# A planned attention-plus-MLP kernel: layer norms, diagonal masks, copies of V and output halves moved between engines, and a new order of all instructions

## The chip, the cores and the metric

The kernel runs on one core of a Trainium2 chip. The metric is the device time of one execution in microseconds (us). It was taken in five runs of the kernel before; the median is 239.56 us, the lowest 237.9 and the highest 241.4. One more execution was recorded by the hardware profiler.

The engines are named as in the profile: PE is TensorE (matmuls), DVE is VectorE, ACT is ScalarE, POOL is GpSimd, and SP issues nearly all transfers. "PEld" is the weight load of PE. "SPq" marks work of SP's queue.

## The reference

```python
x = A_x                                  # 2048 x 512, bf16
xn = layernorm(x)
out = x + A(xn, wq, wk, wv, wo, beta) + silu(xn @ w1) @ w2      # w1: 512 x 1792

# A: 32 heads of 16 columns; 4 segments of 512 rows, one after the other
q, k, v = xn @ wq, xn @ wk, xn @ wv      # split by head and segment
M, z = 0, 0
for s in range(4):
    p = softmax(qs @ ks.T / 4 + causal mask)      # inside the segment
    a_dot = p @ vs
    a_mem = (phi(qs) @ M) / (phi(qs) @ z + 1e-6)  # phi(t) = t + 1 if t > 0 else exp(t)
    o_s = g * a_mem + (1 - g) * a_dot             # g = sigmoid(beta)
    M, z = M + phi(ks).T @ vs, z + sum(phi(ks))
A = concat(o_s) @ wo
```

## The kernel before

**Order.** The kernel does not run its steps in the order in which they are written. `Plan.build` makes the operations, each with an engine, an occupancy and a latency in ns, the data it reads and writes, and a rank out of the list `PRIO` (1,162 numbers). `Plan.schedule` (L1071) plays them through a small model of the five engines and four PSUM banks and writes down one fixed order; each engine's queue then holds its instructions in that order, with semaphores between engines. So every change of a cost or a rank can change the order of the whole kernel. The model has a rule for DVE and POOL: an operation of DVE marked `port` that starts while POOL is busy is prolonged to the end of POOL's operation, and the reverse (L1137 to L1145).

**Front.** x of segment 0 is loaded in two halves, then wk, wq, wv, w1, x of segment 1, w2 and wo (L353 to L362). While these come, PE runs 51 products of an identity (`warm`, L446). The layer norm (`ln`, L454) takes tiles of 128 rows: `bn_stats` and `bn_aggr` on DVE (L477, L478) for mean and variance, or, for tile 3 of segment 0, three activations on ACT (L461 to L468); adding eps and raising to -0.5 on POOL (L486, L489); the normalization itself on DVE (L496). Segment 0 is transposed by PE (L508) and copied out of PSUM by ACT (L520), with 6 filling products behind each transposition; the others are transposed by a DMA (L525).

**Attention.** Head dimension 16 lets four heads share PE, in four row groups. One set of scores fills a PSUM tile `psS` of 128 x 2048 (four banks), of which there is a single one: PE writes scores (L686), ACT takes the exponential of all 2048 columns into a bf16 tile (L697), and only then may PE write the next scores. There are 64 such rounds (16 groups of eight heads times four) and 8 more for the half tiles at the diagonal, two groups at a time (`halves`, L806, with the exponential at L832 into the single buffer `Pd`). The causal part of each diagonal block is zeroed on POOL by `affine_select`: two of 128 x 256 for each of the 64 (L703), and four for each of the 8, of which two cover 64 and two cover 128 partitions, 1024 columns each (L840).

P times V runs in four column groups (L717) with a column of ones in V, so that row 16 of each group is the softmax's sum. V is kept as 16 pairs of heads, 2 heads of a pair, 16 + 1 columns (`K.V`); `low` copies the lower 64 rows of one head of each pair into VA (L608) and of the other into VB (L609), on DVE, 16 times. The two results of a group are copied out of PSUM by DVE into `No` (L749) and `N` (L753); the last `N` alone is copied by ACT.

**Division.** SP's queue gathers the rows of sums (L763) and merges `No` into `N` (L774). DVE inverts the sums and multiplies by the gate (`rc`, L784 and L785); a store to DRAM (L794) and a replicating load (L802) spread the reciprocals over partitions, and DVE multiplies (L964, or L953 in segment 0). The same is done for the memory's denominator (L866 to L870, L877, L885, L890).

**The rest.** q and k are copied out of PSUM by DVE (L543, L584); POOL makes masked copies of k (`kTo`, L548, L556). phi takes ACT (exp, L618), POOL (min, L622) and DVE (L628, with a running sum for k). w1's products go through tanh on ACT (L648) and a product on DVE (L654) into hT; w2 and wo are products of 14 and 4 steps, all issued by a helper (L91 with the full array, L96 in column groups).

```python
op("PE", 222, 228, sc, tau(n) - 700, ..., w=[("psS", n)], mode="R", kind="S")
K.nc.scalar.activation(out=pt(K)[:], in_=K.psS[:], func=AF.Exp, scale=SCALE)      # L697
K.nc.gpsimd.affine_select(out=a, in_=a, compare_op=ALU.is_ge, fill=0.0, base=64 * h,
                          pattern=[[0, 16], [1, 64]], channel_multiplier=-1)      # L840
```

## Time and profile before

| | |
|---|---|
| five runs | 241.4, 237.9, 239.56, 239.55, 239.59 us; median 239.56 |
| the profiled execution's own time | 237.94 us, 1.62 below that median |
| its span, first to last instruction | 236.0 us, so 1.94 us lie around it |
| granted TensorE clock | 1.000 |
| DVE busy | 189.5 us of the span (80%), 336 instructions |
| bytes moved | 18.70 MB; HBM read 11.53 MB, written 2.33 MB |
| SP's queue | rows of issues cover 160.9 us of 236.0 |

How to read it: "busy" is the union of an engine's instructions. Consecutive instructions of ACT, and of DVE, overlap a little in the record, since the end of one is written while the next has begun. In a timeline row the columns are start, duration (both us), engine, line, operation, what it writes and reads, shape, count, and in brackets the idle time before it and what ended that. A row with a count of several merges neighbours. An instruction that cannot get what it needs after it was issued is shown as longer, not as waiting.

### The profile page before, as it was taken

To read this page: it belongs to the slowest core of one execution; us is meant where nothing else is said; L and a number is where in the kernel's file an instruction comes from. 1 tells how busy PE (TensorE), PEld (TensorE's weight loads), DVE (VectorE), ACT (ScalarE), POOL (GpSimd) and SP (SyncE) were. 2 spreads that over 40 slices of the span, in tenths; PEclk is the share of its full clock that TensorE was granted. 3 is DMA by queue.
4 is the path that set the end of the run, shared out by engine and by line. 5 is a ranking of instruction groups with operands and counts; after the bars stand their busy time and mean duration, and the time that the engine had idled before them with its cause. 6 is when DMAs were issued, how large, how long until landed. Compare 5 with 4: busy or idle time off the path is not lost.

```text
span 236.0 us, 8073 instructions
## 1 busy us (share of the span) xinstructions
PE 219.5 (93%) x3378; PEld 104.5 (44%) x3378; DVE 189.5 (80%) x336; ACT 182.6 (77%) x169; POOL 147.9 (63%) x290
## 2 busy tenths in 40 slices
PE   7798979999989999979995999999989999999994
PEld 6733334454344444443441445443434444445541
DVE  3489998999888799699799788979898587783741
ACT  4469999898998999968994768898878889891112
POOL 3389898997956986676767273698739543830000
PEclk9999999999999999999999999999999999999999
DMA  6999451221230211131312212210211200231202
GB/s 195 353 373 267 108 70 31 52 27 37 49 56 19 92 29 35 45 110 57 72 29 52 96 37 68 58 47 10 77 62 40 83 15 15 74 97 36 82 25 89
DMA packets 29356, 18.70 MB, mean 79 GB/s; under 512 B 15753, under 2 KB 28809, under 8 KB 29321
## 3 DMA queue, kind: packets, MB, share of 16 engines
q1 hardware_dynamic: 29176, 18.07, 28.6%
q8 instruction: 26, 0.43, 0.7%
q10 hardware_dynamic: 144, 0.13, 0.2%
q14 instruction: 10, 0.07, 0.2%
HBM read 11.53 MB, written 2.33 MB: 59 GB/s over the span
## 4 chain that ended last, share of the span: by engine, by line
PE 46%; DVE 18%; DMA 12%; POOL 7%; SPq 6%; ACT 5%; issue 5%; DVEq 0%; ACTq 0%
PE psb__216 L91 9%; PE psb__214 L91 7%; PE psb__215 L91 6%; DMA x_all<-in_A_x_dram 5%; PE psS L686 5%; PE psb__217 L91 5%; PE psb__215 L96 3%; PE psb__217 L96 2%; SPq L774 2%; DVE rq L785 2%; DMA xnT__89<-xn__87 1%; DVE zr L784 1%; SPq L763 1%; PE psb__216 L96 1%; DMA mrep__189<-dmem__212 1%
## 5 line engine op out<-in xcount | busy, mean ns | idle before, releaser
L840 POOL TENSOR_SCALAR_AFFINE_SELECT Pd__148<-Pd__148 128x1024 bf16<-128x1024 bf16 (+1 forms) x32 | 36.6, 1153 | 8.8 <-ACT Pd__148 L832 8.4
L91 PEld LDWEIGHTS <-w 128*128 128x128 bf16 x169 | 15.3, 98 | 20.6 <-issue 4.3
L697 ACT ACTIVATE Pt__141<-psS 128x2048 bf16<-128x2048 f32 x10 | 18.8, 1880 | 2.9 <-PE psS L686 2.8
L697 ACT ACTIVATE Pt__147<-psS 128x2048 bf16<-128x2048 f32 x9 | 16.9, 1880 | 3.1 <-PE psS L686 2.5
L697 ACT ACTIVATE Pt__146<-psS 128x2048 bf16<-128x2048 f32 x9 | 16.9, 1882 | 2.5 <-PE psS L686 1.9
L697 ACT ACTIVATE Pt__144<-psS 128x2048 bf16<-128x2048 f32 x9 | 16.9, 1880 | 2.2 <-PE psS L686 2.1
L697 ACT ACTIVATE Pt__142<-psS 128x2048 bf16<-128x2048 f32 x9 | 16.9, 1875 | 2.1 <-PE psS L686 2.1
L697 ACT ACTIVATE Pt__145<-psS 128x2048 bf16<-128x2048 f32 x9 | 16.9, 1881 | 0.9 <-PE psS L686 0.7
L697 ACT ACTIVATE Pt__143<-psS 128x2048 bf16<-128x2048 f32 x9 | 16.9, 1877 | 0.7 <-PE psS L686 0.5
L832 ACT ACTIVATE Pd__148<-psS 128x2048 bf16<-128x2048 f32 x8 | 15.0, 1876 | 3.1 <-PE psS L822 2.3
L703 POOL TENSOR_SCALAR_AFFINE_SELECT Pt__147<-Pt__147 128x256 bf16<-128x256 bf16 x18 | 8.2, 470 | 7.0 <-ACT Pt__147 L697 7.0
L703 POOL TENSOR_SCALAR_AFFINE_SELECT Pt__141<-Pt__141 128x256 bf16<-128x256 bf16 x20 | 8.8, 458 | 5.7 <-ACT Pt__141 L697 5.7
L648 ACT ACTIVATE th__170<-psb__217 128x512 bf16<-128x512 f32 x7 | 4.2, 600 | 9.6 <-PE psb__217 L96 9.5
L703 POOL TENSOR_SCALAR_AFFINE_SELECT Pt__143<-Pt__143 128x256 bf16<-128x256 bf16 x18 | 7.6, 438 | 6.1 <-ACT Pt__143 L697 6.0
L703 POOL TENSOR_SCALAR_AFFINE_SELECT Pt__145<-Pt__145 128x256 bf16<-128x256 bf16 x18 | 8.0, 466 | 4.8 <-ACT Pt__145 L697 4.8
L703 POOL TENSOR_SCALAR_AFFINE_SELECT Pt__146<-Pt__146 128x256 bf16<-128x256 bf16 x18 | 7.2, 417 | 4.8 <-ACT Pt__146 L697 4.8
L91 PE MATMUL psb__214<-xnT__89,w 128*128 128x512 bf16 x32 | 9.1, 380 | 1.1 <-DVE hT__150 L654 0.7
L703 POOL TENSOR_SCALAR_AFFINE_SELECT Pt__144<-Pt__144 128x256 bf16<-128x256 bf16 x18 | 7.3, 424 | 4.4 <-ACT Pt__144 L697 4.4
L703 POOL TENSOR_SCALAR_AFFINE_SELECT Pt__142<-Pt__142 128x256 bf16<-128x256 bf16 x18 | 7.6, 435 | 3.2 <-ACT Pt__142 L697 3.2
L96 PEld LDWEIGHTS <-w 128*32 128x32 bf16 x220 | 5.6, 97 | 4.6 <-issue 0.4
L449 PE MATMUL psS<-ident 128*128 128x128 bf16 x75 | 6.3, 250 | 1.4 <-POOL pm L388 1.4
L91 PE MATMUL psb__217<-xnT__90,w 128*128 128x512 bf16 x27 | 7.5, 381 | 0.0
(817 smaller groups left out, 739.5 us busy)
## 6 DMA issues: line engine op xcount, KB each, us to landing
w<-in_B_w_dram SPq DMA_DIRECT2D x2, 1792.0 KB
x_all<-in_A_x_dram SPq DMA_DIRECT2D x8, 256.0 KB
out_dram<-x_all SPq DMA_DIRECT2D x15, 128.0 KB
wk<-in_A_wk_dram SPq DMA_DIRECT2D x1, 512.0 KB
wq<-in_A_wq_dram SPq DMA_DIRECT2D x1, 512.0 KB
wv<-in_A_wv_dram SPq DMA_DIRECT2D x1, 512.0 KB
wo<-in_A_wo_dram SPq DMA_DIRECT2D x1, 512.0 KB
mrep__189<-dmem__211 SPq DMA_DIRECT2D x2, 128.0 KB
```

What stands on the lines that cost most here:

```text
L91: K.nc.tensor.matmul(out, lhsT=lhsT, rhs=rhs, start=start, stop=stop, skip_group_check=True)
L96: K.nc.tensor.matmul(out[32 * g : 32 * g + 32], lhsT=lhsT[:, 32 * g : 32 * g + 32], rhs=rhs, start=start, stop=stop, tile_position=(0, 32 ...
L449: K.nc.tensor.matmul(K.psS[:, 0, 0:P], lhsT=K.ident[:], rhs=K.ident[:], start=True, stop=True)
L648: K.nc.scalar.activation(out=K.th[g % RING["th"]][:], in_=K.bank(t)[:, :], func=AF.Tanh, scale=0.5)
L686: K.nc.tensor.matmul(K.psS[:, g, c : c + L - q0], lhsT=K.kTo[b][r0:r1, kt, 64:192] if par else K.kT[b][r0:r1, kt * P : kt * P + P], rhs=K. ...
L697: K.nc.scalar.activation(out=pt(K)[:], in_=K.psS[:], func=AF.Exp, scale=SCALE)
L703: K.nc.gpsimd.affine_select(out=a, in_=a, compare_op=ALU.is_ge, fill=0.0, base=64, pattern=[[0, 4], [1, 64]], channel_multiplier=-1,)
L763: K.nc.sync.dma_start(out=zt[r : r + 13 : 4, :], in_=src[DH : DH + 97 : 32, 256 * b : 256 * b + 256],)
L774: K.nc.sync.dma_start(out=K.N[nN][r : r + 16, :], in_=K.No[nNo][r - 16 : r, :])
L785: K.nc.vector.tensor_scalar(out=K.rq[0:nr, :], in0=K.zr[0:nr, :], scalar1=K.gcol[0:nr, dts[0] // 3 : dts[0] // 3 + 1], scalar2=None, op0=A ...
L832: K.nc.scalar.activation(out=pd(K)[:], in_=K.psS[:], func=AF.Exp, scale=SCALE)
L840: K.nc.gpsimd.affine_select(out=a, in_=a, compare_op=ALU.is_ge, fill=0.0, base=64 * h, pattern=[[0, 16], [1, 64]], channel_multiplier=-1,)
```

## The change

Work is moved between engines, some constants of the planner are changed, and the order comes from a new `PRIO`:

- First layer norm (segment 0): ACT takes the statistics of tile 1 in place of tile 3; eps is added on DVE; the four normalized tiles have four buffers (two of them the later `oT`) in place of two; tile 2's copy out of PSUM goes to DVE; 47 warming products in place of 51, and 6, 4, 4, 4 filling ones.
- Layer norms of segments 1 to 3: the normalization is one activation on ACT with scale and bias from columns; POOL makes the bias (`shift`) with one small product for each tile.
- The diagonal masks of `halves`: two DVE products for each pair with a 128 x 64 mask `tri` (made once by POOL), repeated over 16 blocks, in place of four `affine_select` on POOL.
- V is kept with the head of the pair ahead of the pair; the copies into VA and VB are 32 transfers on SP's queue in place of 32 copies on DVE.
- All copies into `N` go to ACT; before, 15 of the 16 were on DVE.
- The two gate products after the reciprocals (`rc`, and the one of the memory's denominator) also write an accumulated sum into an unused column `junk`.
- w1 is loaded in two halves; w2, wo and beta are issued after the first k has been copied out.
- The planner: many occupancies and latencies differ by some per cent to some tens of per cent (a masked `halves` score 240 in place of 440 ns, transfers' latencies 1,350 to 1,800 in place of 2,100 to 2,300 ns); a `port` operation of DVE that meets a busy POOL is put aside until POOL's operation, and those marked `port=3` that are queued behind it, have ended.
- `PRIO` is another list of numbers, and so the order of all engines' queues is another.

```diff
-WARM = 51
-FILL = (6, 6, 6, 6)
+WARM = 47
+FILL = (6, 4, 4, 4)
...
+def xn0(K, t):
+    return K.xn[t] if t < 2 else K.oT[t - 2]
...
-        load([("w1",)], ld_w("w1", "B_w1"), 5, 11500)
-        load([("x", 1, 0)], ld_x(1, 0), 6, 12000)
-        load([("x", 1, 1)], ld_x(1, 1), 7, 12500)
-        load([("w2",)], ld_w("w2", "B_w2"), 8, 17000)
-        load([("wo",)], ld_w("wo", "A_wo"), 9, 18000)
+        for h in range(2):
+            load([("w1", h)], ld_w("w1", "B_w1", slice(h * F // 2, (h + 1) * F // 2)), 5 + h, 8500 + 2500 * h)
+        load([("x", 1, 0)], ld_x(1, 0), 7, 11000)
+        load([("x", 1, 1)], ld_x(1, 1), 8, 11500)
+        for i, (name, src) in enumerate((("w2", "B_w2"), ("wo", "A_wo"))):
+            op("SP", 600, 9000 + 3000 * i, ld_w(name, src), 20000 + i, r=[("kT", 0)], w=[(name,)])
...
-        op("SP", 1600, 2300, beta, 30000, w=[("bcol",)], not_before=26500)
+        op("SP", 1900, 6000, beta, 19000, r=[("kT", 0)], w=[("bcol",)])
...
+        def tri(K):
+            K.nc.gpsimd.memset(K.tri[:], 1.0)
+            for n, base in ((P, 64), (64, 0)):
+                K.nc.gpsimd.affine_select(
+                    out=K.tri[0:n, :], in_=K.tri[0:n, :], compare_op=ALU.is_ge, fill=0.0, base=base,
+                    pattern=[[1, 64]], channel_multiplier=-1,
+                )
+        op("POOL", 500, 120, tri, 15500, r=[("kTo", 0, 1)], w=[("tri",)])
...
-            if s == 0 and j == 3:
+            if s == 0 and j == 1:
...
-                op("ACT", 1400, 170, mean, base, r=[("x", s, 1)], w=[("mv", s, j)])
+                op("ACT", 1660, 170, mean, base, r=[("x", s, 0)], w=[("mv", s, j)])
...
+            if s == 0:
+                def eps(K, t=t):
+                    K.nc.vector.tensor_scalar(
+                        out=K.rstd[:, t : t + 2, 0], in0=K.mv[:, t : t + 2, 1], scalar1=EPS,
+                        scalar2=None, op0=ALU.add,
+                    )
+                op("DVE", 70, 130, eps, base + 2000 + 700 * j, r=[("mv", s, j), ("mv", s, j + 1)],
+                   w=[("veps", s, j)])
...
+                if s > 0:
+                    K.nc.gpsimd.tensor_tensor(
+                        out=rs, in0=K.mv[:, t : t + 2, 1], in1=K.lnc[:, 0:2], op=ALU.add
+                    )
                 K.nc.gpsimd.tensor_tensor(out=rs, in0=rs, in1=K.lnc[:, 2:4], op=ALU.pow)
...
+                if s > 0:
+                    for u in (t, t + 1):
+                        K.nc.gpsimd.tensor_scalar(
+                            out=K.shift[:, u : u + 1], in0=K.mv[:, u, 0:1], scalar1=K.rstd[:, u, 0:1],
+                            scalar2=-1.0, op0=ALU.mult, op1=ALU.mult,
+                        )
+            op("POOL", 1270 if s else 520, 150, rstd, base + 2200 + 700 * j,
+               r=([("mv", s, j), ("mv", s, j + 1)] if s else [("veps", s, j)]) + [("lnc",)],
...
+            def norm1(K, j=j, t=t):
+                K.nc.scalar.activation(
+                    out=K.xn[t % RING["xn"]][:], in_=K.x_all[:, t % XT, :], func=AF.Identity,
+                    scale=K.rstd[:, t, 0:1], bias=K.shift[:, t : t + 1],
+                )
+            if s == 0:
+                op("DVE", 322, 190, norm, base + 2500 + 700 * j, port=1,
+                   r=[("x", s, j // 2), ("mv", s, j), ("rstd", s, j)], w=[("xn0", t)])
+            else:
+                op("ACT", 525, 170, norm1, base + 2500 + 700 * j,
+                   r=[("x", s, j // 2), ("mv", s, j), ("rstd", s, j)], w=[("xn", t)])
...
+                    if j == 2:
+                        K.nc.vector.tensor_copy(out=dst, in_=src)
+                    else:
+                        K.nc.scalar.copy(out=dst, in_=src)
+                op("DVE" if j == 2 else "ACT", 590, 150, ev, base + 3000 + 700 * j,
...
-            def low(K, j=j):
-                b = (4 * s + j) % RING["V"]
-                K.nc.vector.tensor_copy(out=K.VA[b][0:64, :, :], in_=K.V[b][0:64, :, 0, :])
-                K.nc.vector.tensor_copy(out=K.VB[b][64:P, :, :], in_=K.V[b][0:64, :, 1, :])
-            op("DVE", 400, 135, low, due + 4000, port=1, r=[("V", 4 * s + j), ("ones", (4 * s + j) % RING["V"])], w=[("VB", 4 * s + j)])
+            for r in range(2):
+                def half(K, j=j, r=r):
+                    b = (4 * s + j) % RING["V"]
+                    K.nc.sync.dma_start(
+                        out=(K.VB if r else K.VA)[b][64 * r : 64 * r + 64, :, :], in_=K.V[b][0:64, r, :, :]
+                    )
+                op("SP", 580, 1700, half, due + 4000, r=[("V", 4 * s + j), ("ones", (4 * s + j) % RING["V"])],
+                   w=[("VB", 4 * s + j, r)])
...
-                f = K.nc.scalar.copy if end else K.nc.vector.tensor_copy
-                f(out=K.N[nN][:], in_=K.bank(tk[0])[:, :])
+                K.nc.scalar.copy(out=K.N[nN][:], in_=K.bank(tk[0])[:, :])
...
-            op("ACT" if end else "DVE", 600, 135, eve, due + 1, r=[("PV", s, dt, 0)], w=[("N", g4, 0)], free=[tk[0]])
+            op("ACT", 480, 160, eve, due + 1, r=[("PV", s, dt, 0)], w=[("N", g4, 0)], free=[tk[0]])
...
-                    scalar2=None, op0=ALU.mult,
+                    scalar2=0.0, op0=ALU.mult, op1=ALU.add, accum_out=K.junk[0:nr, :],
...
-            for h in range(2):
-                def mask(K, di=di, h=h):
-                    a = pd(K)[0 : P if h else 64, :, :].rearrange("p g (j d q) -> p (g j) d q", d=2, q=64)
-                    a = a[:, :, di, :]
-                    K.nc.gpsimd.affine_select(
-                        out=a, in_=a, compare_op=ALU.is_ge, fill=0.0, base=64 * h,
-                        pattern=[[0, 16], [1, 64]], channel_multiplier=-1,
-                    )
-                op("POOL", 1120, 130, mask, tau(n) + 3500 + 5000 * di, r=[("Pd", pr, 0)],
-                   w=[("Pd", pr, 1 + 2 * di + h)], kind="mask")
+            def mask(K, di=di):
+                a = pd(K)[:, :, :].rearrange("p g (j d q) -> p (g j) d q", d=2, q=64)[:, :, di, :]
+                K.nc.vector.tensor_tensor(
+                    out=a, in0=a, in1=K.tri[:, :].unsqueeze(1).broadcast_to([P, 16, 64]), op=ALU.mult
+                )
+            op("DVE", 600, 135, mask, tau(n) + 3500 + 5000 * di, r=[("Pd", pr, 0), ("tri",)],
+               w=[("Pd", pr, 1 + di)], port=1)
...
-                out=K.rec[:], in0=K.zf[:], scalar1=K.gcol[:, 2:3], scalar2=None, op0=ALU.mult
-            )
-        op("DVE", 1650, 135, ev, port=2, due= tau(NQ * s + DUE["den"][s] + 0.3), r=[("psD", s), ("gcol",)], w=[("rec", s)],
+                out=K.rec[:], in0=K.zf[:], scalar1=K.gcol[:, 2:3], scalar2=0.0, op0=ALU.mult,
+                op1=ALU.add, accum_out=K.junk[:],
...
-    K.V = ring("V", [P, H // 2, 2, DH + 1], BF16)
+    K.V = ring("V", [P, 2, H // 2, DH + 1], BF16)
```

## The prediction

> **What bounds the kernel now.** I read the busy shares first, then the table by stretches from the first exponential to the last, then ACT's timeline, then the timelines of the places where ACT stops, then the groups that the change removes. The page's engine shares:
>
> ```profile
> PE 219.5 (93%) x3378; PEld 104.5 (44%) x3378; DVE 189.5 (80%) x336; ACT 182.6 (77%) x169; POOL 147.9 (63%) x290
> ```
>
> No engine but PE looks full, and a busy PE is not one at its peak. The stretches before, between and after the exponentials (13.68 is the start of the first, 211.5 the end of the last; the columns are PE, PEld, DVE, ACT, POOL):
>
> ```profile
> 0.00:13.68 13.68, 10.82 (x141) 9.16 (x142) 6.43 (x14) 5.92 (x11) 5.29 (x25) 1.00 0.85 291
> 13.68:211.50 197.82, 187.94 (x2830) 84.36 (x2832) 172.08 (x307) 172.70 (x152) 141.85 (x263) 1.00 0.27 67
> 211.50:236.00 24.50, 20.70 (x420) 10.94 (x412) 10.99 (x17) 3.94 (x7) 0.78 (x2) 1.00 0.18 57
> ```
>
> In the middle, three engines are between 87% and 95%. Its clock is the single score tile: exponential, scores, exponential. ACT's timeline shows the fastest beat:
>
> ```profile
> 18.98 1.88 ACT L697 ACTIVATE Pt__143<-psS 128x2048 bf16<-128x2048 f32 x1
> 20.75 0.59 ACT L648 ACTIVATE th__170<-psb__214 128x512 bf16<-128x512 f32 x1
> 21.40 1.88 ACT L832 ACTIVATE Pd__148<-psS 128x2048 bf16<-128x2048 f32 x1
> ```
>
> From 18.98 to 21.40 the beat is 2.42 us, and the 0.59 us of tanh cost nothing, since PE writes scores meanwhile. Over the 71 intervals between the 72 exponentials I counted the small ACT operations in each. None: 13 intervals, median 2.43 us. One: 43, median 2.45. Two: 12, median 2.77. Three: 3, the shortest 3.25. So the first filler is free, each further one costs 0.33 to 0.5. All 71 sum to 195.9; six of them last 3.90 to 5.45 and hold 12.3 us over the fastest common beat of 2.38. Those six are what can be won. The worst is at 124.9:
>
> ```profile
> 122.04 3.43 POOL L840 TENSOR_SCALAR_AFFINE_SELECT Pd__148<-Pd__148 64x1024 bf16<-64x1024 bf16 x3 [0.54 <-ACT Pd__148 L832]
> ...
> 123.96 3.48 DVE L785 TENSOR_SCALAR rq<-zr,gcol 64x256 bf16<-64x256 f32 x1
> ...
> 124.86 1.88 ACT L697 ACTIVATE Pt__142<-psS 128x2048 bf16<-128x2048 f32 x1 [0.51 <-PE psS L686]
> ...
> 125.43 0.78 POOL L703 TENSOR_SCALAR_AFFINE_SELECT Pt__141<-Pt__141 128x256 bf16<-128x256 bf16 x2
> 126.16 1.14 POOL L840 TENSOR_SCALAR_AFFINE_SELECT Pd__148<-Pd__148 128x1024 bf16<-128x1024 bf16 x1
> ...
> 127.38 0.67 DVE L600 CAST V__127<-psb__215 128x512 bf16<-128x512 f32 x1
> ...
> 128.10 0.38 PE L91 MATMUL psb__215<-w,hT__163 128*128 128x512 bf16 x1 [2.76 <-DVE V__127 L600]
> ```
>
> POOL works off a train of selects without a gap, 4.57 us of it L840. DVE's L785, 0.34 us elsewhere, lasts 3.48 and ends with the train. V, behind it on DVE, comes late, PE has no PSUM bank and stands 2.76, and the next exponential starts at 130.3. At 102.4 it is the same with L890 (2.62 in place of 0.42) and 1.56 us of PE.
>
> **The change part by part.** The sum is made against the profiled execution, 237.94 us (span 236.0); the median of the runs is 1.62 above it, and I carry the difference over to the median.
>
> *Masks of the halves.* Removed from POOL: 32 selects, 36.7 us:
>
> ```profile
> L840 POOL TENSOR_SCALAR_AFFINE_SELECT Pd__148<-Pd__148 64x1024 bf16<-64x1024 bf16 x16 | 18.5, 1161 | 4.2 <-ACT Pd__148 L832 4.0
> L840 POOL TENSOR_SCALAR_AFFINE_SELECT Pd__148<-Pd__148 128x1024 bf16<-128x1024 bf16 x16 | 18.2, 1145 | 4.6 <-ACT Pd__148 L832 4.4
> ```
>
> Added on DVE: 16 products of 128x1024 bf16. No row has that shape with a repeated operand. L890, 128x512 bf16, takes 0.42; L980, whose one operand is f32 in PSUM, 0.68. Doubling the columns gives between 0.69 (the part above a start of 0.15 doubled) and 1.22. I take 0.69, since all three tensors are bf16 in SBUF as in L890: 11.0 us, at most 19.5.
>
> *The gate products with an accumulator.* What they gain is the wait. Lower bound of one L785: 0.34 as in the undisturbed rows; upper: 3.48 again. The nearest accumulating row is L628 for k, 0.68 alone and up to 1.09 beside POOL, so a wait of 0.4 may remain. I take 0.8. Even if it still waits, 4.57 of the 5.4 us it waited behind are no longer POOL's. So PE's 2.76 at 128.1 goes: -2.8 (0 to -3.1). The Trainium skill, "SBUF — State Buffer", section "Who interferes with whom", says that tensor_scalar in the form that writes its accumulator does not take the port pair shared with GpSimd; by that the wait would be nil and the gain 3.1, while the same section says that a product with two SBUF inputs does contend, which speaks against the new masks. No row of this trace has the accumulating tensor_scalar.
>
> *The L890 stall at 102.4.* The train there is one L840 (1.32), two masks (0.78) and L927 (1.15). I take half of PE's 1.56: -0.8 (0 to -1.6).
>
> *Relief of DVE and POOL.* Off DVE: 32 copies, 10.3 us; 15 copies into N, 10.2; 12 normalizations (16 take 9.1, the first four 1.7), 7.4; 3.2 of stalls in L785. On it: 11.0 of masks, 0.7 for tile 2. DVE goes from 189.5 to about 170, POOL from 147.9 to about 116 (24 small bias products at 0.2, as L486, are in it). The other four long beats (43.1, 135.5, 145.9, 165.3) have 7.4 us in all; they wait for k's masked copy on POOL (L548 stretched to 1.35 at 138.3), for a q behind statistics on DVE, or for P times V ahead of the scores. Half of them is of the kind that this relieves: -3.7 (0 to -7.4).
>
> *Load on ACT.* Added inside the middle: 15 copies (0.59 each, as L753 on ACT) and 12 normalizations. L461, no column operand, takes 0.63, L468 with one 0.72; with two I take 0.81. Fillers go from 76 to 103. There are 13 empty beats and 11 of one filler that last 2.75 or more; three of these are holes that I close, so 21 places are free. The other 6 cost 0.33 each, 2.0, and the longer normalizations 12 x 0.09, 1.1: +3.0 together (0 if all find room, +10.0 if none does: 27 x 0.33 + 1.1). The Trainium skill, "ScalarE: Activation LUTs", section "Rules for kernel authors", has products and sums done on VectorE and not on ScalarE, and so speaks against this part. In the rows the normalization is 0.41 on DVE and some 0.8 on ACT; by the rule all 27 moves lose, +10 in place of +3.
>
> *V's copies on SP's queue.* 32 issues at 0.54 (L763), 17.3 us; the queue's rows go from 160.9 to 178. A copy lands about 2.2 us after its V (issue plus the 1.5 to 1.7 of the transfers of `zs` and `N` in the chain of waits), in place of 0.5. It is hidden: V of segment 0 is ready at 15.1 to 27.4 and P times V starts only after four exponentials and the halves. If that cover is gone, a transposition or a gather of sums behind it on SP waits for V: 0.5 to 2 us, once a segment. I take 0.
>
> *Front.* ACT's three activations (4.44 to 6.25) can start with the first half at 3.79, but eps is now on DVE, behind three statistics that end at 6.29; the first POOL add was at 5.65. So the first rstd comes about 0.5 later, the second about 0.2 sooner (no add on POOL). The copies out of PSUM then end sooner by one of 0.55, as DVE takes one. Zero (-0.5 to +0.4). w1's first half needs no wait: PE stood 0.37 for w1 at 15.61: -0.3. The warming products shrink by 4 x 0.084; the clock was granted in full with a pause of 1.45 behind them, and I cost this at nothing.
>
> *Order.* A new `PRIO` has no price in the trace. Its bounds: 0, and the six long beats anew, +12.3; I keep half of four of them already.
>
> Sum: -0.3 - 2.8 - 0.8 - 3.7 + 3.0 = -4.6. Profiled: 233.3; against the median: 235.0.
>
> **The rivals.**
>
> *ACT becomes the bound.* All 27 fillers fall into beats that have one: -7.6 + 10.0 = +2.4, so 242.0 and beyond it if holes stay; with half of the relief gone too (+1.9), 243.9. It decides from 20 fillers in full beats, (7.6 - 1.1) / 0.33. For it: ACT is 95% busy or more from 20 to 45 in the table by stretches, where a segment's additions fall. Against it: from 105 to 150 ACT has 11 us idle. Place it at 243.
>
> *New holes for old.* The order breaks elsewhere; only the lock at 124 goes: -0.3 - 2.8 + 3.0 = -0.1, 239.5.
>
> *All holes go.* -0.3 - 12.3 + 3.0 = -9.6: 230.0. For it: outside the six long beats the mean beat is 2.61, (195.9 - 26.6) / 65, so PE and DVE keep up with that elsewhere. Against it: a fixed order meets delays that no plan holds.
>
> **How the numbers follow.** Forecast 0.48 (its own range 232.5 to 238, from the bounds of the relief and of ACT); all holes 0.20; new holes 0.16; ACT the bound 0.16. A difference under 1% (237.2 to 242.0) is about what a measurement of this kernel cannot tell from none. Faster by over 1%: 0.41 of the forecast, all of the 0.20 and 0.05 of new holes, 0.66. Within: 0.07, 0.10 and 0.03 of ACT, 0.20. Slower: 0.13 of ACT and 0.01, 0.14. The range leaves out the half of the 0.20 below 229.5 and ACT's 0.10 above 242: 229.5 to 242.
>
> **What would show it.** Right: no L785 above 1 us; PE never waits over 2 us for DVE; the longest beats under 3.9 us and the middle near 193; DVE near 170, POOL near 116, ACT near 198 us. Wrong: masks of 1.2 us; many beats of 2.8 with two fillers and few empty ones; a beat above 4 us that ends on an instruction that was moved (a normalization or N's copy on ACT, a copy of V on SP); SP late with sums or transposes; or a longer tail, which I left at 24.5.

## The result

The kernel after takes 240.76 us in the median (44 runs, 238.01 to 245.05), the kernel before 239.77 beside it (79 runs). The ratio is 1.0052, interval [1.003, 1.0073]: about 1.2 us slower. Ratios and intervals, here and below, count only the executions that were not in a slower state (28 of the 44), so they need not be quotients of the medians. The forecast was 235.0, that is 4.6 us below the 239.56 it started from. The range held the time; the direction was wrong. A difference under 1%, which is what came, had a chance of 0.20.

Shares of busy time in the profile of after (span 238.9, clock 0.991):

```profile
PE 222.2 (93%) x3347; PEld 105.8 (44%) x3347; DVE 170.3 (71%) x304; ACT 196.5 (82%) x195; POOL 114.7 (48%) x271
```

Every engine's load is what the working had: DVE near 170, ACT near 198, POOL near 116. The groups of the new instructions say the same; columns after the bar are busy us in all and mean ns of one:

```profile
L887 DVE TENSOR_TENSOR Pd__151<-Pd__151,tri 128x1024 bf16<-128x1024 bf16 x16 | 12.0, 768 | 1.9 <-POOL tri L412 1.9
L537 ACT ACTIVATE xn__90<-x_all,shift,rstd 128x512 bf16<-128x512 bf16 x6 | 5.0, 830 | 0.5 <-DMA xnT__93<-xn__90 0.5
L834 DVE TENSOR_SCALAR_CACHE_REDUCE rq<-zr,gcol 64x256 bf16<-64x256 f32 x3 | 1.4, 472 | 0.1
```

The masks are short (0.67 to 0.69 for one that nothing delays, 0.77 in the mean), a normalization on ACT is 0.8, and the gate product (now L834) is 0.47 and never 3.48. So the work was priced rightly, and the time still did not fall. The stretches before, between and after the exponentials show where:

```profile
0.00:13.98 13.98, 11.37 (x130) 9.45 (x131) 7.32 (x17) 5.85 (x11) 4.47 (x23) 1.00 0.82 275
13.98:215.66 201.68, 190.98 (x2834) 86.72 (x2833) 151.47 (x269) 187.08 (x179) 109.44 (x247) 0.99 0.29 72
215.66:238.90 23.24, 19.89 (x392) 9.61 (x383) 11.54 (x20) 3.56 (x7) 0.78 (x2) 0.98 0.21 66
```

The middle is 201.7 in place of 197.8, the tail 1.3 shorter. The two profiles differ by 2.9 us, more than the 1.2 of the ratio; the profile of before kept the full clock, that of after holds a dip of the clock worth some 1.7, shown below. Over the fastest common beat of 2.38, the 71 intervals between exponentials hold 30.8 us (before 26.9). Those of 3.5 us or less hold 14.2 (before 14.6) although they carry 19 of the 27 added ACT operations: the new order found room for these. The longer ones hold 16.6 (before 12.3). The old holes at 102 and 124 are gone, and there are new ones, at 21.3 (5.97 us), 35.4 (6.08), 89.8 (4.84), 94.7 (4.51), 118.1 (4.08) and 124.6 (4.09; not the old one, since no gate product stands there).

The one at 21.3, in the timeline of after:

```profile
10.33 6.65 SPq L354 DMA_DIRECT2D wo<-in_A_wo_dram  x1
...
17.03 2.91 SPq L376 DMA_DIRECT2D bcol<-in_A_beta_dram  x3
...
21.33 1.88 ACT L881 ACTIVATE Pd__151<-psS 128x2048 bf16<-128x2048 f32 x1
...
24.51 0.52 ACT L439 ACTIVATE gcol<-bcol 64x1 f32<-64x1 bf16 x3 [1.31 <-DMA bcol<-in_A_beta_dram]
...
24.93 0.80 ACT L537 ACTIVATE xn__91<-x_all,shift,rstd 128x512 bf16<-128x512 bf16 x1
...
26.51 0.69 DVE L887 TENSOR_TENSOR Pd__151<-Pd__151,tri 128x1024 bf16<-128x1024 bf16 x1 [1.93 <-POOL tri L412]
...
27.30 1.85 ACT L747 ACTIVATE Pt__147<-psS 128x2048 bf16<-128x2048 f32 x1
```

beta is issued behind wo, whose issue occupies SP for 6.65 us, and lands at 24.5. The gate's tanh waits for it at the head of ACT, with two normalizations and two tanh ahead of the exponential behind it; the scores were there at 23.65, the exponential starts at 27.30. DVE meanwhile waits for `tri`. The longest hole, at 35.4, has no late data ahead of its exponential:

```profile
35.41 1.88 ACT L747 ACTIVATE Pt__150<-psS 128x2048 bf16<-128x2048 f32 x1
...
37.34 0.40 PE L736 MATMUL psS<-qT__107,kT__95 16*128 16x320 bf16 x8
...
37.66 0.82 ACT L537 ACTIVATE xn__90<-x_all,shift,rstd 128x512 bf16<-128x512 bf16 x1
...
41.03 0.61 ACT L802 CAST N__174<-psb__217 128x512 bf16<-128x512 f32 x1
41.49 1.92 ACT L747 ACTIVATE Pt__144<-psS 128x2048 bf16<-128x2048 f32 x1
```

The scores were there at 37.74, and ACT worked without a pause until 41.49: eight small operations stand ahead of the exponential, four tanh, one of phi, two normalizations and a copy into `N`. Only the last three were moved. In all eight kernels made from after the beat here lasts 5.9 to 8.2, also where the moved operations are off ACT (5.94 in a_nact). So the order makes this hole, and no run removes it.

The hole at 89.8, with SP's queue ahead of it:

```profile
76.35 0.51 SPq L656 DMA_DIRECT2D VA__134<-V__128  x1
76.96 0.55 SPq L656 DMA_DIRECT2D VB__138<-V__126  x1
...
81.44 0.58 SPq L656 DMA_DIRECT2D VB__139<-V__127  x1
82.12 0.54 SPq L843 DMA_DIRECT2D drec__208<-rq  x1
82.70 3.66 SPq L823 DMA_DIRECT2D N__177<-No__180  x4
86.46 0.66 SPq L851 DMA_DIRECT2D rep__197<-drec__208  x1
...
89.13 1.23 SPq L619 DMA_TRANSPOSE phiK<-phiKT__113  x1
...
93.21 0.23 PE L95 MATMUL psb__220<-V__130,phiK 128*128 128x128 bf16 x1 [1.86 <-DMA phiK<-phiKT__113]
```

SP's rows follow one another from 73.9 to 90.4, with no more than 0.2 us between two. Seven of them are copies of V. phiKT was ready at 86.2; its transposition is issued at 89.13 and lands at 93.2. PE waits 1.86, and then its clock falls; the table by stretches (the third figure from the end is the granted clock):

```profile
89.80:94.10 4.30, 2.26 (x21) 1.26 (x20) 3.01 (x7) 2.88 (x3) 0.89 (x2) 1.00 0.63 87
94.10:98.90 4.80, 4.80 (x24) 1.67 (x27) 2.08 (x4) 2.88 (x3) 3.31 (x5) 0.64 0.08 21
```

A clock of 0.64 for 4.8 us is 1.7 us of PE. The hole at 94.7 lies in this dip.

### The profile page after: what moved, and what is told of

It is laid out like the page before. It is cut to its first block, busy times and chain, and to the rows that moved or that the text cites. A ratio compares the mean times of both kernels' runs of the same rounds, so it can differ in the third digit from the quotient of the medians.

```text
span 238.9 us, 8066 instructions
## 1 busy us (share of the span) xinstructions
PE 222.2 (93%) x3347; PEld 105.8 (44%) x3347; DVE 170.3 (71%) x304; ACT 196.5 (82%) x195; POOL 114.7 (48%) x271
## 4 chain that ended last, share of the span: by engine, by line
PE 48%; ACT 14%; DMA 12%; SPq 11%; issue 6%; DVE 4%; POOL 3%; ACTq 0%; DVEq 0%; POOLq 0%
PE psb__218 L95 7%; PE psb__219 L95 6%; PE psb__220 L95 6%; PE psb__217 L95 6%; SPq L354 5%; PE psS L736 5%; DMA bcol<-in_A_beta_dram 3%; DMA xnT__93<-xn__90 3%; ACT Pd__151 L881 2%; PE psb__220 L100 2%; ACT Pt__150 L747 2%; PE psb__218 L100 2%; PE psO__4150 L100 2%; PE psO__4153 L100 2%; PE psO__4152 L100 2%
## 5 line engine op out<-in xcount | busy, mean ns | idle before, releaser
L753 POOL TENSOR_SCALAR_AFFINE_SELECT Pt__147<-Pt__147 128x256 bf16<-128x256 bf16 x18 | 8.4, 483 | 13.0 <-ACT Pt__147 L747 13.0
L753 POOL TENSOR_SCALAR_AFFINE_SELECT Pt__145<-Pt__145 128x256 bf16<-128x256 bf16 x18 | 7.3, 429 | 14.7 <-ACT Pt__145 L747 14.6
L753 POOL TENSOR_SCALAR_AFFINE_SELECT Pt__144<-Pt__144 128x256 bf16<-128x256 bf16 x20 | 7.9, 417 | 11.7 <-ACT Pt__144 L747 11.7
L887 DVE TENSOR_TENSOR Pd__151<-Pd__151,tri 128x1024 bf16<-128x1024 bf16 x16 | 12.0, 768 | 1.9 <-POOL tri L412 1.9
L753 POOL TENSOR_SCALAR_AFFINE_SELECT Pt__149<-Pt__149 128x256 bf16<-128x256 bf16 x18 | 7.3, 426 | 11.7 <-ACT Pt__149 L747 11.7
L753 POOL TENSOR_SCALAR_AFFINE_SELECT Pt__146<-Pt__146 128x256 bf16<-128x256 bf16 x18 | 7.5, 436 | 9.4 <-ACT Pt__146 L747 9.3
L753 POOL TENSOR_SCALAR_AFFINE_SELECT Pt__148<-Pt__148 128x256 bf16<-128x256 bf16 x18 | 7.4, 435 | 8.3 <-ACT Pt__148 L747 8.3
L753 POOL TENSOR_SCALAR_AFFINE_SELECT Pt__150<-Pt__150 128x256 bf16<-128x256 bf16 x18 | 7.5, 436 | 7.5 <-ACT Pt__150 L747 7.5
L1108 ACT ACTIVATE x_all<-psO__4151 128x512 bf16<-128x512 f32 x1 | 0.6, 597 | 11.1 <-PE psO__4151 L100 11.1
L95 PEld LDWEIGHTS <-wq 128*128 128x128 bf16 x55 | 5.0, 101 | 6.7 <-issue 2.6
```

Of the source, the lines that this page charges most:

```text
L95: K.nc.tensor.matmul(out, lhsT=lhsT, rhs=rhs, start=start, stop=stop, skip_group_check=True)
L887: K.nc.vector.tensor_tensor(out=a, in0=a, in1=K.tri[:, :].unsqueeze(1).broadcast_to([P, 16, 64]), op=ALU.mult)
L1108: K.nc.scalar.activation(out=K.x_all[:, t_ % XT, :], in_=K.psO[j][:, :], func=AF.Copy, scale=0.5)
```

## The experiments

All sixteen kernels keep the order of the kernel they are made from: only bodies of steps are changed, unless the diff says so. A step that goes to another engine stands where the order had it; in no run does the planner order the moved parts anew with the old list. Names with b_ are made from the kernel before, those with a_ from after. Ratios are to the kernel before on the same chip; a hundredth is 2.4 us. For b_masks only three executions of before stand behind the ratio, hence its wide interval.

| kernel | ratio | interval |
|---|---|---|
| b_accum: before + accumulating gate products | 0.980 | 0.9765 to 0.9833 |
| b_masks: before + masks on DVE | 0.986 | 0.9757 to 0.9965 |
| b_accum_masks: both | 0.984 | 0.9803 to 0.9875 |
| b_act: before + N copies, normalizations on ACT | 1.020 | 1.0163 to 1.0235 |
| b_vdma: before + V's copies on SP | 1.023 | 1.0179 to 1.0283 |
| b_vdma_x: the same, one x load ahead of copies | 1.021 | 1.0177 to 1.0236 |
| b_vpool: the same copies issued by POOL | 1.011 | 1.0078 to 1.0133 |
| **b_all: order of before, all four parts** | **1.044** | 1.0404 to 1.0485 |
| **a_none: order of after, none of the four** | **1.047** | 1.0414 to 1.0516 |
| after | 1.005 | 1.003 to 1.0073 |
| a_unmask: after, masks back on POOL | 1.023 | 1.0165 to 1.03 |
| a_unaccum: after, plain gate products | 1.003 | 0.9982 to 1.0078 |
| a_nact: after, N copies, normalizations on DVE | 1.011 | 1.0062 to 1.0149 |
| a_vdve: after, V's copies on DVE | 0.998 | 0.9947 to 1.0002 |
| a_gate: after, gate 40 us later | 1.000 | 0.996 to 1.004 |
| a_gate_vdve: both | 0.993 | 0.9891 to 0.9975 |
| a_undo: a_gate_vdve + a_nact | 1.009 | 1.0066 to 1.012 |

**Accumulating gate products (b_accum).**

```diff
-                    scalar2=None, op0=ALU.mult,
+                    scalar2=0.0, op0=ALU.mult, op1=ALU.add, accum_out=K.junk[0:nr, :],
```

> The kernel before, its order kept, with only the gate products of the two reciprocals writing an accumulated sum too. The prediction's term: L785 at 124 goes from 3.48 to 0.5 to 0.9 us and PE's wait of 2.76 behind it goes, span -2.8, ratio 0.988. If the accumulating form waits for POOL as well: 1.00. If the time is only lost a little later for another reason (POOL's train itself is late): 0.995 to 1.00.

Measured 0.980, 4.8 us, more than any of its expectations. The timeline of b_accum at the stall of 102 and at the place of the old lock:

```profile
102.47 2.62 DVE L891 TENSOR_TENSOR phiQ__118<-phiQ__118,mrep__191 128x512 bf16<-128x512 bf16 x1
...
122.12 3.41 POOL L840 TENSOR_SCALAR_AFFINE_SELECT Pd__149<-Pd__149 64x1024 bf16<-64x1024 bf16 x3 [0.56 <-ACT Pd__149 L832]
...
124.02 0.47 DVE L785 TENSOR_SCALAR_CACHE_REDUCE rq<-zr,gcol 64x256 bf16<-64x256 f32 x1
...
124.43 0.68 DVE L600 CAST V__128<-psb__216 128x512 bf16<-128x512 f32 x1
```

POOL's train of selects is the same, and L785 runs through it in 0.47. V is copied at 124.43 and not at 127.38. From the exponential at 124.9 to the next, 3.0 us are won in the profile (2.45 in place of 5.45). Another 0.9 is won near 173, but not at a gate product: in before, DVE's L890 waits there for a load of `mrep`, and the same 0.9 is won in b_act and b_vdma, whose gate products are plain. The stall at 102 stays, 2.62 as before; it is a plain product of two tensors and no gate product. So 3.0 of the 4.8 us are the lock's; the rest is not shown to be the accumulator's. The row at 124.02 agrees with the Trainium skill, "SBUF — State Buffer", section "Who interferes with whom", on the form that writes its accumulator.

**N's copies and normalizations on ACT (b_act).**

```diff
-                f = K.nc.scalar.copy if end else K.nc.vector.tensor_copy
-                f(out=K.N[nN][:], in_=K.bank(tk[0])[:, :])
+                K.nc.scalar.copy(out=K.N[nN][:], in_=K.bank(tk[0])[:, :])
...
+                if s > 0:
+                    K.nc.scalar.activation(
+                        out=K.xn[t % RING["xn"]][:], in_=K.x_all[:, t % XT, :], func=AF.Identity,
+                        scale=K.rstd[:, t, 0:1], bias=K.shift[:, t : t + 1],
+                    )
+                    return
```

> The kernel before, its order kept, with only the load on ACT of the change: the 15 copies into N and the 12 normalizations of segments 1 to 3 run on ACT, at the places in the order that they had on DVE, and POOL makes the bias columns. Theory A: 27 operations at 0.33 to 0.6 us in an order that did not provide for them, +6 to +12 us, ratio 1.025 to 1.05. Theory Q: ACT has the room (13 empty beats, six long ones), DVE is relieved of 17 us: 0.995 to 1.01.

Measured 1.020, 4.8 us slower, between the two theories; 5.0 us are lost by 63 us. ACT's timeline in b_act:

```profile
27.05 1.90 ACT L708 ACTIVATE Pt__146<-psS 128x2048 bf16<-128x2048 f32 x1
28.81 0.84 ACT L502 ACTIVATE xn__88<-x_all,shift,rstd 128x512 bf16<-128x512 bf16 x1
29.51 0.62 ACT L659 ACTIVATE th__170<-psb__217 128x512 bf16<-128x512 f32 x1
29.99 1.91 ACT L708 ACTIVATE Pt__147<-psS 128x2048 bf16<-128x2048 f32 x1
31.75 0.64 ACT L659 ACTIVATE th__171<-psb__215 128x512 bf16<-128x512 f32 x1
32.23 0.86 ACT L502 ACTIVATE xn__89<-x_all,shift,rstd 128x512 bf16<-128x512 bf16 x1
32.93 0.68 ACT L629 ACTIVATE ek__123<-kT__94 128x512 bf16<-128x512 bf16 x1
33.45 1.93 ACT L708 ACTIVATE Pt__148<-psS 128x2048 bf16<-128x2048 f32 x1
```

No row has a wait: ACT is the bound here, with beats of 2.94 and 3.46 in place of 2.38 and 2.77.

**V's copies on SP (b_vdma), one load moved (b_vdma_x), another issuer (b_vpool).** The three kernels, the second on top of the first, the third in place of it:

```diff
-                K.nc.vector.tensor_copy(out=K.VA[b][0:64, :, :], in_=K.V[b][0:64, :, 0, :])
-                K.nc.vector.tensor_copy(out=K.VB[b][64:P, :, :], in_=K.V[b][0:64, :, 1, :])
+                for r in range(2):
+                    K.nc.sync.dma_start(
+                        out=(K.VB if r else K.VA)[b][64 * r : 64 * r + 64, :, :], in_=K.V[b][0:64, r, :, :]
+                    )
```

```diff
+        for o in self.order:
+            if o.kind == "load" and o.start > 60000:
+                past = [t for t in lows if o.start - 9000 < t <= o.start]
+                if past:
+                    to = max([min(past) - 1] + [d.start + 1 for d in o.deps])
+                    o.start = min(o.start, to)
```

```diff
-                    K.nc.sync.dma_start(
+                    K.nc.gpsimd.dma_start(
```

> The kernel before, in its own order, with nothing changed but V's copies: V kept with the head of the pair ahead of the pair, and 32 transfers on SP's queue in place of 32 copies on DVE. Theory (the queue takes what DVE gives back): DVE falls by 10.3 us to about 179, SP's rows of issues rise by about 17 us, and transpositions that stand behind eight such copies on SP land 4 us later once a segment: 0 to +3 us, ratio 1.000 to 1.012, with a beat of more than 3.9 us or a wait of PE for phiK that the kernel before does not have. Rival (my prediction's step: the copies are hidden, and DVE's relief shows): -0.5 to -2 us, ratio 0.992 to 0.998.

> The kernel before with V's copies by 32 transfers on SP, as in the run of that part alone (1.023), and one more edit: the one load of x that stood behind four of these copies on SP's queue near 117 us is put ahead of them. Theory (the loss is the queue: x late, DVE's statistics waiting at the head of DVE, N's copy out of PSUM behind them, PE without a bank): x issued 2.4 us sooner, DVE's wait of 4.3 us down to about 2, the beat of 8.1 us down to about 5.7, ratio 1.009 to 1.016. Rival (the copies' own traffic, or another wait, takes its place): ratio 1.020 to 1.026.

> The kernel before with V's copies by the same 32 transfers, issued by POOL and not by SP. Theory (what costs is the place on SP's queue, not the transfers): SP's rows as in the kernel before, x issued before 113 us, no beat of 8 us at 119; POOL pays for 32 issues, which the trace has not priced on that engine; ratio 0.995 to 1.012. Rival (a transfer is simply later than a DVE copy, whoever issues it, or POOL's issues stretch its other work and DVE's): 1.015 or above.

b_vdma took 1.023, 5.5 us slower and more than either theory said. Its timeline at the dearest place:

```profile
115.17 0.54 SPq L609 DMA_DIRECT2D VA__132<-V__126  x1
...
117.03 0.59 SPq L609 DMA_DIRECT2D VB__137<-V__125  x1
...
117.67 0.59 SPq L340 DMA_DIRECT2D x_all<-in_A_x_dram  x1
...
122.26 0.69 DVE L477 BATCH_NORM_STATS2 stats__84<-x_all 128x6 f32<-128x512 bf16 x1 [4.32 <-DMA x_all<-in_A_x_dram]
...
123.08 0.66 DVE L755 CAST N__173<-psb__216 128x512 bf16<-128x512 f32 x1
...
123.79 0.59 PE L91 MATMUL psb__216<-w,hT__163 128*128 128x512 bf16 x1 [3.98 <-DVE N__173 L755]
...
127.11 1.88 ACT L834 ACTIVATE Pd__148<-psS 128x2048 bf16<-128x2048 f32 x1 [5.71 <-PE psS L824]
```

This is a chain over four engines: x stands behind V's copies on SP; the statistics that want x stand at the head of DVE; N's copy, which wants nothing of x, stands behind them; PE has no bank; the exponential waits 5.71. In b_vdma_x x was issued at 115.20 and N copied at 120.64, and the beat of 8.08 us was gone. Yet the ratio only fell to 1.021: another transposition behind SP's rows cost 6.37 us near 70 (5.07 before that edit), and the lock of L785 near 125, which the long beat had covered, came back. The theory of the queue is right for the place, wrong in its size for the whole. In b_vpool nothing of this comes; one hole of 6.84 us at 32.6 does, where POOL issues a copy behind its selects, and PE waits for it:

```profile
35.36 0.23 PE L719 MATMUL psb__216<-Pd__148,VB__137 128*17 128x64 bf16 x4 [2.71 <-DMA VB__137<-V__125]
```

So a transfer is not hidden or dear in itself; what it costs is what it stands behind and what stands behind it.

**The masks (b_masks, b_accum_masks).**

```diff
-                    K.nc.gpsimd.affine_select(
-                        out=a, in_=a, compare_op=ALU.is_ge, fill=0.0, base=64 * h,
-                        pattern=[[0, 16], [1, 64]], channel_multiplier=-1,
-                    )
+                    K.nc.vector.tensor_tensor(
+                        out=a, in0=a, in1=K.tri[:, :].unsqueeze(1).broadcast_to([P, 16, 64]), op=ALU.mult
+                    )
```

> The kernel before, in its own order, with the accumulating gate products and with the diagonal masks of the halves as 16 DVE products (mask made once on POOL at the start). POOL falls by about 36 us to 112, DVE rises by 11 less the stalls. Theory (the masks on POOL cost a half of the 7.4 us of the other long beats and of the stall at 102): 1 to 4 us below the accumulating products alone, ratio 0.965 to 0.977, with no stall of the product of the memory's division at 102. Rival (once the gate products no longer wait for POOL, POOL's masks are off the path, and the DVE products are as long as what they replace): 0.977 to 0.985, no different from 0.980.

> The kernel before, in its own order, with only the diagonal masks as 16 DVE products; the gate products keep their old form. With the accumulator alone this order took 0.980, with both 0.984. In the new order the plain gate product lasted 0.34 to 0.47 us, not 3.5, once the masks were off POOL. Theory (two remedies for one stall: the plain product has no train of selects to wait for, and the pause of PE at 128 goes without the accumulator): L785 below 1 us, ratio 0.979 to 0.990. Rival (POOL's other work still holds the product, or the masks' 11 us on DVE cost what the selects did): L785 stretched over 1 us, ratio 0.995 or above.

Alone 0.986, together with the accumulator 0.984, the accumulator alone 0.980: two remedies for one stall, whose gains do not add. With both, the product at 102 takes 0.42 and its beat is 1.6 us shorter, but the beats at 13.5, 70.1 and 124.0 are 0.4 to 1.2 longer than in b_accum, and that is lost again. The four other long beats of before (4.08, 4.64, 4.32 and 3.90) are 4.08, 4.64, 4.32 and 3.89 with both: POOL's selects did not hold them. The plain gate product in b_masks:

```profile
124.54 1.46 POOL L709 TENSOR_SCALAR_AFFINE_SELECT Pt__142<-Pt__142 128x256 bf16<-128x256 bf16 x2 [2.83 <-ACT Pt__142 L703]
124.77 0.35 DVE L791 TENSOR_SCALAR rq<-zr,gcol 64x256 bf16<-64x256 f32 x1
```

It lasts 0.35, since there is no train to wait for; the two selects beside it take 1.46, where others take 0.78.

**All parts without the order, the order without the parts (b_all, a_none).** b_all joins the edits above; a_none undoes all four in after and moves the gate later.

> All four moved parts at once in the order of the kernel before: accumulating gate products, diagonal masks as DVE products, the copies into N and the normalizations of segments 1 to 3 on ACT, V's copies by SP's queue. What the kernel after has beside them is its front and its order. Theory (the parts cost what they cost alone, and the new order has earned some of it back): -4.8 + 0.9 + 4.75 + 5.5 = +6.3 us from the separate runs, ratio 1.018 to 1.032. Rival (the losses of ACT's load and of SP's queue fall into the same beats, and the order of after earns nothing): 1.000 to 1.012, no different from the kernel after.

> The kernel after, in its own order, with all four moved parts undone and the gate's operation later: masks by four POOL selects, gate products without an accumulator, N's copies and the normalizations on DVE, V's copies on DVE. What stays of the change is its front and its order. Theory (an order fits the parts it was made with): slower than the kernel before by 1.5 to 4 us, ratio 1.010 to 1.030, with gate products stretched behind trains of selects. Rival (the new order is as good as the old for the old parts): 0.995 to 1.005.

1.044 and 1.047, both beyond their expectation. Together the parts cost 10.6 us in the old order, and the new order, without the parts it was made with, costs 11.1. Added up, the separate runs make +6.3, but that sum counts one gain three times: the beat at the lock, 5.45 in before, is 2.45 in b_accum, 2.38 in b_act and 2.37 in b_vdma. These two gains of 3.1 too many are more than the 4.3 by which b_all is above the sum, so it is not shown that the parts hinder one another. The granted clock over the span was below full in all six executions of each (0.979 to 0.993; before beside them 0.990 to 1.000), and how much of the loss is that is not shown either.

**Parts undone in the new order (a_unmask, a_unaccum, a_nact, a_vdve, a_gate, a_gate_vdve, a_undo).** The edits are the reverse of those above; the gate is moved by

```diff
+        for o in self.order:
+            if o.kind == "gate":
+                o.start = 62000
```

> The kernel after, in its own order, with only the diagonal masks back on POOL (four selects for each pair, at the places of the two products in the new order; the gate products keep their accumulator). Undoing masks and gate products together cost 3.7% in this order (1.047 against 1.009), in the order of before only 1.6%. Theory (in the new order the masks carry it, since POOL's place for 36.7 us of selects has been filled with other work): +4 to +8 us against the kernel after, ratio to the kernel before 1.020 to 1.040. Rival (the accumulator carries it here too): 1.003 to 1.012.

> The kernel after, in its own order, with only the gate products back to the form without an accumulator. Theory (what these products wait for is a train of selects, and that train has gone with the masks): they last 0.5 to 1.3 us, 0 to +1.5 us against the kernel after, ratio to the kernel before 1.003 to 1.012. Rival (the lock comes whatever POOL does): stretches over 2 us, ratio 1.015 or above.

> The kernel after, in its own order, with the 15 copies into N and the 12 normalizations back on DVE, each at the place in DVE's queue that the order gives by its new rank; POOL's 12 small products for the bias stay in, unused. ACT falls by about 18.7 us to 178, DVE rises by about 14 to 184. Theory (the load on ACT cost +4.75 in the order of before and costs as much here): -3 to -5 us against the kernel after, ratio to the kernel before 0.983 to 0.993. Rival (the new order is built around that load, and the longer beats come from its early gate and its queue on SP): within 1 us of the kernel after, ratio 1.001 to 1.009, with beats of two and three fillers fewer but the beats at 21, 35 and 95 us still over 4 us.

> The changed kernel with one part undone and every queue's order kept: the 32 copies of V into VA and VB are DVE copies again, at the places in the order where their transfers stood. Theory Q (SP's queue is the new bound: its rows follow each other without a gap from 62 to 96 us, eight copies of V among them, and the transposition of phi(k) that PE waits for at 91 comes late): the long beats at 72.8, 89.8 and 94.7 shrink, PE's wait of 1.9 for phiK goes and with it the stretch at half clock, the span falls by 3 to 5 us to 234 to 236, ratio to the kernel before 0.985 to 0.995. Theory A (the 27 operations moved to ACT are what is paid): nothing changes or it is slower, since DVE gets back 7.7 us of work: 1.005 to 1.015.

> The changed kernel with one operation moved: the gate's three tanh on ACT and the POOL operations behind them stand about 40 us later in the order (they are first needed after 70 us). In the changed kernel they hold ACT for 1.3 us at 23.2, waiting for beta, with the next exponential queued behind. Theory Q: the beat at 21.3, 5.97 us long, loses 1.3 to 1.8, and as the later waits are not tied to it the span falls by 1 to 2 us: ratio 0.997 to 1.002. Theory A: the beat is as long, since two normalizations and two tanh stand there too: 1.005.

> The kernel after, in its own order, with the two early or queued things undone that were the dearest in it: the gate's operation some 40 us later, V's copies on DVE. All else stays. Alone they gave 0.995 and 0.992 of the kernel after. Theory (they cost in different places, 21 us and 76 to 99 us): ratio to the kernel before 0.988 to 0.996, so a kernel with the change's other parts and its order is faster than before by about 1%. Rival (both only removed the same dip of the clock at 94 to 99 us, or the next wait takes their place): 0.997 to 1.003.

> The kernel after with three parts undone at once: the gate's operation some 40 us later, V's copies on DVE, the 15 copies into N and the 12 normalizations on DVE. What stays of the change: masks as DVE products, the accumulating gate products, the new front, the new order. Theory (the parts that lose are the load on ACT and the load on SP, and what is left gains): ratio 0.975 to 0.988, that is 233 to 236 us, near the kernel before with accumulating gate products alone (0.980). Rival (the loss is in the order itself): 0.995 or above, with long beats at 35 and 118 us unchanged.

Masks on POOL cost 4.3 us more than after, and the accumulator is worth nothing (1.003 against 1.005): the reverse of the old order's picture, where the accumulator did as much alone as with the masks. In a_unmask a hole opens where POOL's selects stand ahead of its small products for the bias:

```profile
28.67 2.35 POOL L888 TENSOR_SCALAR_AFFINE_SELECT Pd__151<-Pd__151 64x1024 bf16<-64x1024 bf16 x2
...
32.09 0.50 POOL L519 TENSOR_SCALAR shift<-mv,rstd 128x1 f32<-128x1 f32 x2
...
32.63 0.81 ACT L537 ACTIVATE xn__91<-x_all,shift,rstd 128x512 bf16<-128x512 bf16 x1 [2.10 <-POOL shift L519]
```

The load on ACT, 4.8 us in the old order, costs nothing in the new: taken off (a_nact), the kernel is not faster than after (1.011 against 1.005, intervals that overlap). My theory there fell. Undoing V's copies wins 0.8%, undoing these and the early gate gives 0.993, faster than before. The early gate alone is not clear of the intervals (1.000 against 1.005): in a_gate the beat at 21 shrank by 1.6 us, and its two neighbours grew by 0.7 and 1.2. a_undo, which takes ACT's load away from a_gate_vdve, goes from 0.993 to 1.009: there the load on ACT is worth 1.6% to the new order. Its expectation failed.

The dip of the clock at 94 was absent in the profiles of a_vdve, a_gate and a_gate_vdve. In a_gate the transposition of phiK still came 1.46 late. These profiles end 2.7 to 4.1 us before that of after, while the ratios differ by 1.2 to 2.9 us. Every execution has its granted clock on record, and this tells how often a dip occurs. Of the 28 executions of after behind the ratio, 17 have 0.997 or more over the span (median 239.2 us) and 11 less (median 240.5); of all 44, 27 have less. With V's copies back on DVE it is 1 of 12 (a_vdve) and 1 of 12 (a_gate_vdve), with the gate alone moved 7 of 12. At full clock, and against the median of before on the same chips, after stands at 0.9975 (239.17 against 239.77) and a_vdve at 0.9976 (238.49 against 239.07). So what V's copies still cost in the new order is, as far as these runs tell, the dip behind the late phiK. Before has dips too, in 65 of the 87 executions beside these runs (medians 238.0 without, 239.0 with); its profile was one without.

The lowest ratio of all is that of b_accum, the kernel before with the accumulator alone, 0.980 of before and some 6 us below after; b_accum_masks and b_masks (0.984, 0.986) cannot be told from it.

## Why the prediction was wrong

- **The order: the step that failed.** "A new `PRIO` has no price in the trace. Its bounds: 0, and the six long beats anew, +12.3; I keep half of four of them already." I priced each part on the beats and holes of the old order and carried the sum to a kernel with another. The old order with the parts is at +10.6 us, the new with them at +1.2: the order, together with the front, is worth -9.4, of the other sign than its bound, and the parts are worth +10.6 in the old order, not -4.6. One half was wrong by 15.2 us, the other by 9.4, and 5.8 was left; that the time still fell into the range is luck. The -9.4 is against the old order as it stood; what a new plan for the parts from the old list would give stays open.
- **V's copies, taken at 0.** I named the price of a lost cover ("0.5 to 2 us, once a segment") and did not use it; in the old order it was 5.5 (with the beat at the lock 3.1 shorter in the same run), in the new 1.8, by way of the clock. I looked only at who waits for V, and that was hidden; what stands behind the copies on SP (x, phiK's and xn's transpositions) paid.
- **Load on ACT, +3.0.** 4.8 in the old order, where the fillers fall into full beats before 63 us; in the new order nothing (a_nact), or a gain of 1.6% once the gate and V's copies are out of the way (a_undo). Empty beats fell from 13 to 5 there, so most found a free place. The count of free places was a count for an order that no longer held. The rule that was cited against this part names products and sums; 15 of the 27 moves are copies.
- **L785, -2.8.** Right, and the mechanism as described: 3.0 at its beat. The run as a whole won 4.8, and the other 1.8 are not shown to come from these products.
- **L890, -0.8.** Its stall is untouched by the accumulator and goes with the masks; its beat then won 1.6, the upper bound, and other beats lost as much.
- **Relief, -3.7.** Failed as a term of the old order. With the accumulator in place, the masks on DVE changed it by +0.9 (0.984 against 0.980, intervals that overlap), and the four long beats kept their length to 0.01 us: they did not wait for POOL's selects. For masks and accumulator I added gains that were two ways to the same gain. In the new order the masks off POOL are worth 4.3.
- **Prices of single operations.** Right: masks 0.67 to 0.69, 0.77 in the mean with two that were delayed (I took 0.69), normalization 0.83 (0.81), gate product 0.47 (0.8 allowed), loads of all engines within 2 us. The bias products are 12 and not 24, at 0.27.
- **Front, -0.3.** Not resolved: the first exponential starts at 13.98 in after, 13.4 to 14.3 over the other profiles, whatever was changed.
- **Rivals.** "New holes for old" (239.5) is what came, at 240.8, though not for its reason: beside the lock it had nothing but the ACT load in the sum. What it lacked were the gate behind beta at 21, the eight operations on ACT at 35 and V's copies at 76 to 93. ACT as the bound is what b_act shows in the old order before 63 us.

## What to carry to other kernels

A kernel whose order is fixed for its costs is not a sum of parts: price a part only in the order in which it will run, and where the order is new, take the bounds of the order on both sides and wide, ahead of the sum of parts. When work moves to a queue, list what stands behind it there and what stands behind the one who waits, over as many engines as the chain has. Two edits that remove the same stall count once, and so does a stall that other edits merely hide; try the smallest alone, since here the accumulator beat the whole.

## What was not expected of the hardware

- **The clock.** PE's wait of 1.86 us at 91.3, in a stretch of 4.30 us with 2.26 busy, was followed by a granted clock of 0.64 over 4.8 us. In before, the wait of 2.76 at 125.3, in a stretch of 4.40 with 1.64 busy, left it at 1.00. The Trainium skill, "TensorE: Matmul & The Clock Gate", section "Why this matters for your kernels", puts the point at gaps of about 3 us; here a shorter one was followed by the dip and a longer one was not, so the length of one gap did not decide. In a_gate a wait of 1.46 at the same place was followed by none, and of the 44 executions of after 17 kept 0.997 or more.
- **Issues on SP.** The issue of a plain copy is 0.5 to 0.6 us in most rows, but wo's lasted 6.65 in after and 8.52 in before, with the transfers ahead of it still moving 371 GB/s (10.3 to 17.0 in after), and beta behind it landed 7.5 us after its first row.
- **A mask repeated by stride.** The product of 128x1024 with a 128x64 operand repeated 16 times ran in 0.67 to 0.69, that of 128x512 without a repetition (L890) in 0.42. Twice the columns took 1.6 times as long; the two rows give a start of 0.16, near the 0.15 that the prediction took. Two of the sixteen were longer, 1.64 at 56.2 and 1.11 at 109.6, both begun while POOL was at work.
